# Attention and routed experts on one core: logits in groups of four pairs, wide products from the second expert on, the last two evictions halved

## The chip, the core and the metric

The kernel runs on one core of a Trainium2 chip. The core has a matrix engine (PE), a vector engine (DVE), a scalar engine (ACT), a general engine (POOL) and a queue engine (SP), and 16 DMA engines that move data between HBM and the on-chip memory. PE writes only to PSUM; ACT and DVE read PSUM and write the on-chip memory. The metric is the device time of one execution in microseconds (us).

## What is computed

Causal attention over 4 batches of 12 heads with 448 tokens and head size 64; its rows are the input `x` of a mixture of 8 experts, in which every expert takes 224 tokens.

```
scores = scale * q @ k.T, masked above the diagonal, softmax over keys
x      = (softmax @ v), heads side by side          # 1792 x 768
logits = x @ w_gate                                 # 1792 x 8
order  = argsort(-logits.flatten())                 # greedy: a token to its best expert
...                                                 # that still has room (224 places)
h      = relu(x[mask] @ w1[e]);  out[mask] = h @ w2[e]
```

## The kernel before

**Attention.** The 48 heads are worked as 24 pairs `pp` (6 in a batch), and a batch's 448 tokens as 4 blocks of 112. `plan` writes PE's order out by hand: in round `n` PE computes the scores of pair `n`, the transposes of the softmax of pair `n-1` (`turns`), for early pairs the transposes of the output rows of pair `n-3` (`rows_at`), what `logits_back` adds, the product with `v` of pair `n-1` (`values`) and what `logits` adds for pair `n-2`. Every PE task hangs on the one before (`self.line`), so this order is fixed. DVE and ACT tasks are placed by a planner that works with estimated durations and priorities; some copies may go to either engine (`ACT/DVE`), whichever the planner finds free. Masking with the row maximum (L228) is DVE's, the exponential (L238) ACT's, and copies from PSUM (L252 on ACT, L254 on DVE) are shared.

**Logits.** `w_gate` stands in `WG` as 32 columns for each pair (16 used). `logits_mm` (L331) multiplies the attention output `XT` of several pairs of one batch, each into its own 32 partitions of one PSUM tile: pairs 0 to 3 in one set, pairs 4 and 5 in another. The result is copied out (`lt`), turned back by four transposes (`logits_tr`, L352), and `logits_ev` multiplies on DVE by the reciprocal sums of the softmax (two instructions, L365) and adds over the pairs (L369, and L371 into `L`). The last two pairs go by `logits_direct` (L340), without the way back. In all there are seven sets: 4, 2, 4, 2, 4, 2, 4 pairs, and the direct one.

**Routing.** When `L` of the first three batches is done (`self.log`), DVE may begin with routing steps of low priority, the list `extras`: an argmax over 12 blocks (L632 to L640), keys (L650 to L660) and six comparisons into `Ge` (L674), which PE then sums in `early_count` (L697). After the last batch the router finds, for one expert after the other, the 224 tokens, by rounds in which DVE compares (L668, L783) and PE counts (L769, L786). While the first expert's tokens are looked for, PE runs products without use (L1147).

**Experts.** A second planner orders the eight experts `p`. POOL gathers the 224 rows of an expert (L1129, into one of two `xio` buffers), PE turns them (L1155), ACT and DVE split them into a high and a low part (`xhl`). Weights come in eight pieces for each expert; ACT casts the high part (`wh`, L1114) and DVE subtracts three times for the low part (`wl`, L1120), up to eight pieces ahead. The first product takes 8 blocks `f` of 6 slices `d` each. Expert 0 does it in full precision. From expert 1 on a slice is high times high, high times low and low times high. Expert 1 computes each with 224 columns (L1192, L1193, L1194) into one sum. Experts from `TWICE` on, 2 and later, take both halves of `xhl` in one product of 448 columns (L1190) and then L1194; ACT then copies out the second sum (`hc`, L1204) and DVE adds the two (`hs`, L1208), before ACT's relu (L1200) and DVE's low part (L1212). The second product (L1224) is evicted by ACT (L1228, 384 columns each) into `xio`, and POOL scatters the rows (L1243). The last expert's second product is ordered so that its two last PSUM tiles (`u` 1, `z` 0 and 1) finish one after the other, each with an eviction and a scatter of its own.

Of the kernel before, what the change touches and what calls it, by code (L numbers as in the profile page):

```python
# [7 lines left out]
F32 = mybir.dt.float32  # L8
# [6 lines left out]
OP = mybir.AluOpType  # L15
# [4 lines left out]
C, NC = 112, 4  # L20
# [11 lines left out]
FILL = 0.217  # L32
BIG = 1.0e30
# [3 lines left out]
TWICE = 2  # L37
# [117 lines left out]
class Attention(Schedule):  # L155
    def __init__(self, ctx, tc, gc, keep, k, qk, vP, wgP, xd, L):
# [10 lines left out]
        self.T, self.lt, self.u = {}, {}, {}  # L167
# [159 lines left out]
    def logits_mm(self, b, half):  # L327
        p0, m = ((0, 4), (4, 2))[half]
        t = self.ps.tile([128, S], F32, name="t", bufs=4)
        for p in range(m):  # L330
            self.nc.tensor.matmul(t[32 * p:32 * p + 32], self.WG[:, p0 + p, :], self.XT[6 * b + p0 + p],  # L331
                                  start=True, stop=True)
        self.T["l"] = t

    def logits_direct(self, pp):
        b, q = divmod(pp, 6)
        if q == 4:
            self.u = self.ps.tile([C, NC, 128], F32, name="t", bufs=4)
        for i in range(NC):
            self.nc.tensor.matmul(self.u[:, i, 32 * (q - 4):32 * (q - 4) + 32], self.XT[pp][:, i * C:i * C + C],  # L340
                                  self.WG[:, q, :], start=True, stop=True)

    def logits_cp(self, e, b, half):
        m = (4, 2)[half]
        self.lt = self.wk.tile([128, S], F32, name="lt", bufs=2)
        self.copy(e, self.lt[:32 * m], self.T["l"][:32 * m])

    def logits_tr(self, b, half):
        m = (4, 2)[half]
        self.u = self.ps.tile([C, NC, 128], F32, name="t", bufs=4)  # L350
        for i in range(NC):
            self.nc.tensor.transpose(self.u[:, i, :32 * m], self.lt[:32 * m, i * C:i * C + C],  # L352
                                     self.k["idf"][:32 * m, :32 * m])

    def logits_ev(self, b, half):
        p0, m = ((0, 4), (4, 2))[half]
        if half == 0:
            self.pl = self.wk.tile([C, NC, E, 14], F32, name="pl", bufs=2)
            self.nc.gpsimd.memset(self.pl[:, :, :, 13:14], 0.0)
        pl = self.pl  # L360
        rs = self.RS[b][:, p0:p0 + m, :2 * NC].rearrange("p r (s i) -> p s i r", s=2)
        u = self.u[:, :, :32 * m].rearrange("p i (r z) -> p i r z", z=32)
        o = 9 * half
        for sd in range(2):
            self.nc.vector.tensor_tensor(pl[:, :, :, o + sd:o + 2 * m:2].rearrange("p i e r -> p i r e"),  # L365
                                         u[:, :, :, sd * E:sd * E + E],
                                         rs[:, sd, :, :, None].to_broadcast([C, NC, m, E]), op=OP.mult)
        if half == 0:
            self.nc.vector.tensor_reduce(pl[:, :, :, 8], pl[:, :, :, :8], axis=AX.X, op=OP.add)  # L369
        else:  # L370
            self.nc.vector.tensor_reduce(self.L[:, b * NC:b * NC + NC, :], pl[:, :, :, 8:14], axis=AX.X, op=OP.add)  # L371
# [6 lines left out]
    def plan(self, rt):  # L378
# [4 lines left out]
        self.line = None  # L383
# [129 lines left out]
    def logits(self, pp):  # L513
# [7 lines left out]
        if q not in (3, 5) or not 0 <= pp < NP:  # L521
            return
        half = q // 4
        p0, m = ((0, 4), (4, 2))[half]
        pr = 5.9 - 0.1 * pp
        t = self.pe(0.77, lambda: self.logits_mm(b, half),
                    [self.xts[6 * b + p0 + u] for u in range(m)] + self.ring("t", 4), 3)
        c = self.add("ACT/DVE", {"ACT": 0.42, "DVE": 0.56}, lambda e: self.logits_cp(e, b, half), [t], pr + 0.3)
        self.rings.setdefault("t", []).append([c])
        self.lts = c  # L530

    def logits_back(self, pp):
        b, q = divmod(pp, 6)
# [756 lines left out]
```

## Time and profile before

| | |
|---|---|
| three runs | 498.94, 499.57, 504.29 us; median 499.57 us |
| the profiled execution | 499.02 us, of which the span from first to last instruction is 497.2 us |
| PE busy | 487.1 us, 98% of the span, granted clock 0.997 on average |
| DVE busy | 381.0 us, 77% |
| ACT busy | 305.4 us, 61% |
| POOL busy | 50.2 us, 10% |

Busy time is summed over overlapping matmuls as a union; a matmul's own duration covers its pipeline, so the distance from one start to the next tells what a matmul costs in a stream.

### The profile page before, as it was taken

How to read it: one execution, taken by the hardware profiler on the slowest of the kernel's cores; microseconds unless marked ns; L12 is line 12 of the kernel's file. 1: busy time of each engine (PE TensorE's matmuls, PEld its weight loads, DVE VectorE, ACT ScalarE, POOL GpSimd, SP SyncE). 2: the span in 40 equal slices, each digit the busy share in tenths (PEclk: the TensorE clock that was granted, in tenths of full speed). 3: DMA queues.
4: the chain of work that ended last, by engine and by line, in shares of the span. 5: the costliest groups of instructions: out<-in, count | busy, mean ns of one | idle time of the engine just before them, and what ended most of it. 6: DMA issues, size and time to landing. Idle time of an engine off the chain costs nothing.

```text
span 497.2 us, 10680 instructions
## 1 busy us (share of the span) xinstructions
PE 487.1 (98%) x3933; PEld 406.3 (82%) x3933; DVE 381.0 (77%) x1292; ACT 305.4 (61%) x786; POOL 50.2 (10%) x87
## 2 busy tenths in 40 slices
PE   8999999999999999999999999999999999999995
PEld 4666666766667676999999999999899999999994
DVE  4878777877789786698999999999998486584510
ACT  4988888879898681344645645563664574664410
POOL 5000000000000011010120110210213110200101
PEclk9999999999999999999999999999999999999998
DMA  8933174127000038686967766582976876682101
GB/s 224 316 99 107 38 248 160 39 86 244 6 3 1 1 120 237 242 250 218 331 204 253 240 193 192 196 286 74 299 248 201 295 246 201 212 274 66 57 1 55
DMA packets 18884, 84.07 MB, mean 169 GB/s; under 512 B 2256, under 2 KB 4816, under 8 KB 18832
## 3 DMA queue, kind: packets, MB, share of 16 engines
q1 hardware_dynamic: 16160, 72.36, 45.1%
q0 software_dynamic: 2672, 11.04, 7.1%
q8 instruction: 31, 0.51, 0.4%
q14 instruction: 21, 0.17, 0.1%
HBM read 72.38 MB, written 11.01 MB: 168 GB/s over the span
## 4 chain that ended last, share of the span: by engine, by line
PE 85%; DVE 4%; DMA 4%; ACT 2%; issue 2%; POOL 2%; POOLq 0%; DVEq 0%; ACTq 0%
PE po L1224 25%; PE ph L1190 11%; PE t L246 10%; PE s L272 10%; PE s L218 7%; PE ph L1194 6%; PE t L218 3%; DMA wr<-in_w 2%; DMA xio<-xd,idx 2%; PE rt L769 2%; PE ph L1185 2%; PE ph L1155 2%; PE t L296 2%; PE t L331 1%; PE ph L1192 1%
## 5 line engine op out<-in xcount | busy, mean ns | idle before, releaser
L1120 DVE TENSOR_TENSOR wl<-wr,wh 128x512 fp32r<-128x512 f32 x180 | 116.6, 683 | 14.9 <-ACT wh L1114 14.9
L1114 ACT CAST wh<-wr 128x1536 fp32r<-128x1536 f32 x60 | 88.8, 1480 | 61.7 <-DMA wr<-in_w 36.3
L238 ACT ACTIVATE P<-Sm,mx 112x224 f32<-112x224 f32 (+2 forms) x192 | 99.1, 523 | 23.2 <-DVE mx L228 23.2
L1190 PE MATMUL ph<-xhl,wh 128*128 128x448 f32 x288 | 94.1, 381 | 0.0
L1194 PE MATMUL ph<-xhl,wl 128*128 128x224 f32 x336 | 89.6, 267 | 0.0
L1224 PE MATMUL po<-wh,HH 128*112 128x384 f32 x256 | 68.3, 343 | 0.0
L1224 PE MATMUL po<-wl,HH 128*112 128x384 f32 x256 | 67.6, 340 | 0.0
L1224 PE MATMUL po<-wh,HL 128*112 128x384 f32 x256 | 67.6, 340 | 0.0
L228 DVE CUSTOM_DVE_ANT_0 Sm<-s,MK 112x448 f32<-112x448 f32 (+1 forms) x144 | 59.7, 464 | 6.5 <-POOL iof L580 5.8
L1194 PEld LDWEIGHTS ph<-xhl,wl 128*128 128x128 f32 x336 | 64.2, 191 | 0.0
L1190 PEld LDWEIGHTS ph<-xhl,wh 128*128 128x128 f32 x288 | 54.1, 188 | 4.8 <-issue 0.4
L246 PE MATMUL t<-idf,P 112*112 112x112 f32 x480 | 52.6, 262 | 0.4 <-ACT P L238 0.4
L272 PE MATMUL s<-PT,v 112*64 112x448 f32 (+3 forms) x384 | 50.6, 405 | 0.0
L246 PEld LDWEIGHTS t<-idf,P 112*112 112x112 f32 x480 | 45.9, 133 | 5.1 <-ACT P L238 1.5
L1224 PEld LDWEIGHTS po<-wl,HH 128*112 128x112 f32 x256 | 43.7, 175 | 0.3
L1224 PEld LDWEIGHTS po<-wh,HL 128*112 128x112 f32 x256 | 43.5, 174 | 0.2
L1224 PEld LDWEIGHTS po<-wh,HH 128*112 128x112 f32 x256 | 43.2, 175 | 0.3
L252 ACT COPY PT<-t 112x448 f32<-112x448 f32 (+1 forms) x109 | 42.7, 465 | 1.2 <-PE t L246 1.1
L218 PE MATMUL s<-raw 64*112 64x112 f32 (+2 forms) x288 | 41.4, 415 | 0.1
L272 PEld LDWEIGHTS s<-PT,v 112*64 112x64 f32 x384 | 23.3, 136 | 21.3 <-issue 10.0
L218 PEld LDWEIGHTS s<-raw 64*112 64x112 f32 x288 | 26.8, 174 | 15.8 <-issue 6.1
L238 ACT ACTIVATION_READ_ACCUMULATOR P<-Sm,mx 112x1 f32 x192 | 37.0, 193 | 0.0
(169 smaller groups left out, 655.1 us busy)
## 6 DMA issues: line engine op xcount, KB each, us to landing
wr<-in_w SPq DMA_DIRECT2D x64, 768.0 KB, 5.2
raw<-in_qk SPq DMA_DIRECT2D x11, 896.0 KB, 10.5
v<-in_v SPq DMA_DIRECT2D x12, 448.0 KB, 6.0
xd<-xio SPq DMA_DIRECT2D x2, 1344.0 KB, 6.5
xd<-xio SPq DMA_DIRECT2D x3, 672.0 KB, 4.1
raw<-in_qk SPq DMA_DIRECT2D x1, 448.0 KB, 4.9
xd<-xio SPq DMA_DIRECT2D x1, 448.0 KB, 3.9
xio<-xd,idx POOLq DMA_INDIRECT x16, 5.0
```

What stands on the lines that cost most here:

```text
L218: self.nc.tensor.matmul(ts[sd][:, o:o + m], q[:, 0, i * C:i * C + C], q[:, 1, :m], start=True, stop=True)
L228: self.nc.vector.tensor_tensor_reduce(Sm[:, QO[i]:QO[i] + m], self.S.pop((pp, sd, i)), self.MK[:, S - m:], -0.125, 3.0e38, OP.add, OP.min, ...
L238: self.nc.scalar.activation(P[:, s], Sm[:, s], AF.Exp, bias=mx[:, i:i + 1], scale=-1.0, accum_out=self.RS[b][:, pr, sd * NC + i:sd * NC + ...
L246: self.nc.tensor.transpose(t[:, o + (i - j) * C:o + (i - j) * C + C], P[:, QO[i] + j * C:QO[i] + j * C + C], self.k["idf"][:C, :C])
L252: self.nc.scalar.copy(out, x)
L272: self.nc.tensor.matmul(self.AV[pp][sd * 64:sd * 64 + 64, j * C:S], self.V[2 * pp + sd][:, j, :], self.PT[pp, sd][:, KO[j]:KO[j] + m], sta ...
L296: self.nc.tensor.transpose(t[:, i * 128:i * 128 + 128], self.XT[pp][:, i * C:i * C + C], self.k["idf"])
L1114: self.nc.scalar.copy(hi, self.R[p, c])
L1120: self.nc.vector.tensor_sub(lo[:, s], self.R[p, c][:, s], hi[:, s].bitcast(F32))
L1190: nc.tensor.matmul(t[:, :2 * CAP], hi[:, s], x[:, d].rearrange("p z t -> p (z t)"), start=d == 0, stop=False)
L1194: nc.tensor.matmul(t[:, :CAP], lo[:, s], x[:, d, 0], start=False, stop=d == 5)
L1224: self.nc.tensor.matmul(self.T[p, "o", u][z][:, :384], a[p][:, f, u * C:u * C + C], w[:, o:o + 384], start=f == 0 and n == 0, stop=f == 7 ...
```

## The change

It does three things. The sets of the logits are no longer cut at batches: `SETS` names runs of four pairs, 0 to 3, 4 to 7, 8 to 11, 12 to 15 and 16 to 19, then pairs 20 and 21, and the direct set 22 and 23. `logits_ev` takes a set apart again where a batch ends or its fifth pair begins. `TWICE` is 1, so expert 1 uses the 448-column product and the two additional steps on ACT and DVE. And the last two evictions are cut into 192 columns for ACT and 192 for DVE.

```diff
+SETS = ((0, 4), (4, 4), (8, 4), (12, 4), (16, 4), (20, 2), (22, 2))
-TWICE = 2
+TWICE = 1
...
-    def logits_mm(self, b, half):
-        p0, m = ((0, 4), (4, 2))[half]
+    def logits_mm(self, p0, m):
         t = self.ps.tile([128, S], F32, name="t", bufs=4)
-        for p in range(m):
-            self.nc.tensor.matmul(t[32 * p:32 * p + 32], self.WG[:, p0 + p, :], self.XT[6 * b + p0 + p],
-                                  start=True, stop=True)
-        self.T["l"] = t
+        for u in range(m):
+            self.nc.tensor.matmul(t[32 * u:32 * u + 32], self.WG[:, (p0 + u) % 6, :], self.XT[p0 + u], start=True, stop=True)
+        self.T["l", p0] = t
...
+    def logits_ev(self, p0, m):
+        parts = [[p0]]
+        for p in range(p0 + 1, p0 + m):
+            if p % 6 in (0, 4):
+                parts.append([])
+            parts[-1].append(p)
+        for ps in parts:
...
+            for sd in range(2):
+                self.nc.vector.tensor_tensor(pl[:, :, :, o + sd:o + 2 * n:2].rearrange("p i e r -> p i r e"),
...
+            if q + n == 4:
+                self.nc.vector.tensor_reduce(pl[:, :, :, 8], pl[:, :, :, :8], axis=AX.X, op=OP.add)
+            elif q + n == 6:
+                self.nc.vector.tensor_reduce(self.L[:, b * NC:b * NC + NC, :], pl[:, :, :, 8:14], axis=AX.X, op=OP.add)
...
-        self.log[b] = d
+                if any(p % 6 == 5 for p in range(p0, p0 + m)):
+                    self.log[pp // 6 if pp % 6 == 5 else pp // 6 - 1] = d
...
             if f == 7:
-                a = [add("ACT", 0.41, lambda p=p, u=u, z=z: self.evict(p, u, z), [prev], 9.0) for z in zs]
+                if p == E - 1 and u == 1:
+                    a = [add(e, 0.3, lambda p=p, u=u, z=z, h=h, c=c: self.evict(p, u, z, h, c), [prev], 9.0)
+                         for z in zs for h, (e, c) in enumerate((("ACT", self.nc.scalar.copy),
+                                                                 ("DVE", self.nc.vector.tensor_copy)))]
+                else:
+                    a = [add("ACT", 0.41, lambda p=p, u=u, z=z: self.evict(p, u, z), [prev], 9.0) for z in zs]
...
+    def evict(self, p, u, z, h=None, copy=None):
+        if h is not None:
+            s = slice(h * 192, h * 192 + 192)
+            copy(self.IO[p][:, 2 + u, z * 384:z * 384 + 384][:, s], self.T[p, "o", u][z][:, s])
+            return
```

Three places in the instruction order. Line numbers of the changed program are up to 13 higher. The first is PE in the round in which the fifth and sixth pair of the first batch had their set (`raw` are q and k, `PT` the turned softmax, `lt` the copied logits). Before:

```order
L272 MATMUL s<-PT,v 64x224 x2
L331 MATMUL t<-xt_265,WG 32x448 x2
L218 MATMUL t<-raw 112x224 x2
L218 MATMUL s<-raw 112x448 x2
L218 MATMUL s<-raw 112x336 x2
L218 MATMUL s<-raw 112x112 x2
L246 MATMUL t<-idf,P 112x112 x20
L296 MATMUL t<-idf,xt_265 112x128 x4
L352 MATMUL t<-idf,lt 112x64 x4
```

And now:

```order
L273 MATMUL s<-PT,v 64x224 x2
L219 MATMUL t<-raw 112x224 x2
L219 MATMUL s<-raw 112x448 x2
L219 MATMUL s<-raw 112x336 x2
L219 MATMUL s<-raw 112x112 x2
L247 MATMUL t<-idf,P 112x112 x20
L297 MATMUL t<-idf,xt_265 112x128 x4
L273 MATMUL s<-PT,v 64x448 x2
```

The product and the four transposes of that set are gone from here; pairs 4 and 5 stand with 6 and 7 two rounds later.

The second place is DVE at the end of attention, from the last reciprocals to the last sums of the logits (`Ge`, `k0f` to `k3f` are early routing steps). Before:

```order
L279 RECIPROCAL rs<-rs 112x9
L254 COPY lt<-t 128x448
L254 COPY PT<-t 112x448
L254 COPY PT<-t 112x224
L365 TENSOR_TENSOR pl<-t,rs 112x4x4x8 x2
L369 TENSOR_REDUCE pl<-pl 112x32
```

And now:

```order
L280 RECIPROCAL rs<-rs 112x9
L654 TENSOR_SCALAR k0f<-m_2216 112x12
L655 TENSOR_TENSOR k1f<-m_2216,k0f 112x12
L662 TENSOR_SCALAR k2f<-k1f 112x12
L664 TENSOR_SCALAR k3f<-k1f 112x12
L678 TENSOR_TENSOR Ge<-m_2216,top 112x256 x5
L255 COPY PT<-t 112x448
L678 TENSOR_TENSOR Ge<-m_2216,top 112x256
L371 TENSOR_TENSOR pl<-t,rs 112x4x2x8 x2
L375 TENSOR_REDUCE pl<-pl 112x32
```

The copy of `lt` went to ACT, and ten early routing steps, which stood one to three rounds earlier, now stand around DVE's last copy of `PT`.

The third place is the end of the program with the semaphores that an instruction waits for in brackets: ACT before, and then ACT and DVE now.

```order
L1204 COPY hc<-ph 128x224 [waits PE_49,Activation_49]
L1200 ACTIVATE HH<-hs 128x224 [waits DVE_49]
L1228 COPY xio<-po_6744 112x384 [waits DMASW4_49,DMASW3_49,DMASW5_49,DMASW2_49,PE_49]
L1228 COPY xio<-po_6745 112x384 [waits PE_49]
L1228 COPY xio<-po_6800 112x384 [waits PE_49]
L1228 COPY xio<-po_6801 112x384 [waits PE_49]
```

```order
L1213 COPY hc<-ph 128x224 [waits PE_49,Activation_49]
L1209 ACTIVATE HH<-hs 128x224 [waits DVE_49]
L1241 COPY xio<-po_6724 112x384 [waits DMASW4_49,DMASW3_49,DMASW5_49,DMASW2_49,PE_49]
L1241 COPY xio<-po_6725 112x384 [waits PE_49]
L1239 COPY xio<-po_6780 112x192 [waits DVE_49]
L1239 COPY xio<-po_6781 112x192 [waits DVE_49]
```

```order
L1217 TENSOR_TENSOR hs<-ph,hc 128x224 [waits Activation_49]
L1221 SCALAR_TENSOR_TENSOR HL<-hs,HH 128x224 [waits Activation_49]
L1239 COPY xio<-po_6780 112x192 [waits DMASW4_49,DMASW3_49,DMASW5_49,DMASW2_49,PE_49]
L1239 COPY xio<-po_6781 112x192 [waits PE_49]
```

The halves on DVE wait for PE; the halves on ACT, which read the same PSUM tile, wait for DVE.

## Rows read from the trace of the kernel before

**Rows 1.** Windows: us; busy PE, PEld, DVE, ACT, POOL; PEclk, DMA share, GB/s

```profile
30.00:60.00 30.00, 30.00 (x248) 19.54 (x246) 23.05 (x93) 24.88 (x87) 0.00 (x0) 1.00 0.21 63
242.00:262.00 20.00, 20.00 (x226) 19.74 (x225) 19.43 (x63) 11.84 (x17) 5.60 (x6) 1.00 0.74 247
```

**Rows 2.** Waits of PE: who for whom, us in total, times, longest

```profile
PE ph L1155 <- DMA xio<-xd,idx: 0.6, 2, 0.4
PE rt L786 <- DVE cd L783: 0.5, 2, 0.3
```

**Rows 3.** Timeline of PE, sets of four and two: start, duration, instruction

```profile
42.60 0.96 PE L331 MATMUL t<-xt,WG 128*32 128x448 f32 x8
43.49 0.64 PE L218 MATMUL t<-raw 64*112 64x224 f32 x4
...
57.55 0.95 PE L331 MATMUL t<-xt,WG 128*32 128x448 f32 x4
58.43 0.64 PE L218 MATMUL t<-raw 64*112 64x224 f32 x4
...
63.20 0.43 PE L352 MATMUL t<-idf,lt 64*112 64x64 f32 x4
63.56 0.97 PE L272 MATMUL s<-PT,v 112*64 112x448 f32 x4
```

**Rows 4.** Timeline of PE, the last set of four turned back, and what follows

```profile
171.26 0.65 PE L352 MATMUL t<-idf,lt 128*112 128x128 f32 x4
171.84 2.11 PE L272 MATMUL s<-PT,v 112*64 112x448 f32 x16
```

**Rows 5.** Timeline of PE, first product of expert 1, then of expert 2

```profile
244.04 0.27 PE L1192 MATMUL ph<-xhl,wh 128*128 128x224 f32 x1
...
246.06 0.30 PE L853 MATMUL rt<-val,oh 112*128 112x2 f16 x6
...
280.53 0.37 PE L1190 MATMUL ph<-xhl,wh 128*128 128x448 f32 x1
...
283.69 0.26 PE L769 MATMUL rt<-A,G 112*128 112x8 bf16 x4
```

**Rows 6.** Groups by line and shape: count, busy us, mean ns, idle before

```profile
L1208 DVE TENSOR_TENSOR hs<-ph,hc 128x224 f32<-128x224 f32 x48 | 18.6, 388 | 19.3 <-ACT hc L1204 18.9
L1204 ACT COPY hc<-ph 128x224 f32<-128x224 f32 x48 | 16.5, 345 | 18.6 <-PE ph L1194 16.5 <-PE rt L781 1.1 <-PE rt L786 0.4
L254 DVE COPY PT<-t 112x448 f32<-112x448 f32 x24 | 15.0, 624 | 5.8 <-PE t L246 5.7
L252 ACT COPY PT<-t 112x448 f32<-112x448 f32 x72 | 33.4, 524 | 1.2 <-PE t L246 1.1
```

**Rows 7.** Groups by line, DVE from 176 to 252.5 us: the subtractions for `wl`

```profile
L1120 DVE TENSOR_TENSOR wl<-wr,wh 128x512 fp32r<-128x512 f32 x27 | 17.4, 680 | 0.3 <-ACT wh L1114 0.3
```

**Rows 8.** Timeline of PE, the second product of expert 1 begins

```profile
260.50 0.41 PE L1224 MATMUL po<-wh,HH 128*112 128x384 f32 x1
```

**Rows 9.** Timeline of DVE at the end of attention

```profile
155.04 1.09 DVE L674 TENSOR_TENSOR Ge<-m,top 112x256 bf16<-112x256 f32 x3
...
169.19 0.21 DVE L279 RECIPROCAL rs<-rs 112x9 f32<-112x9 f32 x1
169.32 0.63 DVE L254 COPY lt<-t 128x448 f32<-128x448 f32 x1
170.58 0.97 DVE L254 COPY PT<-t 112x448 f32<-112x448 f32 x2 [0.64 <-PE t L246]
```

**Rows 10.** Timeline: the halved copy in attention, and the program's end

```profile
174.02 0.35 ACT L252 COPY xt<-s 128x224 f32<-128x224 f32 x1 [2.28 <-PE s L272]
174.40 0.39 DVE L254 COPY xt<-s 128x224 f32<-128x224 f32 x1 [1.40 <-ACT xt L252]
491.33 0.48 ACT L1228 COPY xio<-po 112x384 f32<-112x384 f32 x1 [3.69 <-PE po L1224]
492.09 0.94 POOL L1243 DMA_INDIRECT out<-xio,idh  x1 [3.14 <-ACT xio L1228]
```

More of the change, by code (lines that the diff above doesn't have):

```diff
@@ L337, in logits_direct @@
         if q == 4:
-            self.u = self.ps.tile([C, NC, 128], F32, name="t", bufs=4)
+            self.u[pp] = self.ps.tile([C, NC, 128], F32, name="t", bufs=4)
+        u = self.u[6 * b + 4]
         for i in range(NC):
-            self.nc.tensor.matmul(self.u[:, i, 32 * (q - 4):32 * (q - 4) + 32], self.XT[pp][:, i * C:i * C + C],
+            self.nc.tensor.matmul(u[:, i, 32 * (q - 4):32 * (q - 4) + 32], self.XT[pp][:, i * C:i * C + C],
                                   self.WG[:, q, :], start=True, stop=True)
[L343 to L346, printed above, removed]
@@ L348, in logits_tr, with logits_cp @@
-    def logits_tr(self, b, half):
-        m = (4, 2)[half]
-        self.u = self.ps.tile([C, NC, 128], F32, name="t", bufs=4)
+    def logits_cp(self, e, p0, m):
+        self.lt[p0] = self.wk.tile([128, S], F32, name="lt", bufs=2)
+        self.copy(e, self.lt[p0][:32 * m], self.T.pop(("l", p0))[:32 * m])
+    def logits_tr(self, p0, m):
+        u = self.u[p0] = self.ps.tile([C, NC, 128], F32, name="t", bufs=4)
         for i in range(NC):
-            self.nc.tensor.transpose(self.u[:, i, :32 * m], self.lt[:32 * m, i * C:i * C + C],
+            self.nc.tensor.transpose(u[:, i, :32 * m], self.lt[p0][:32 * m, i * C:i * C + C],
@@ L520, in logits @@
             return
[L521 to L530, printed above, removed]
@@ L532, in logits_back @@
-    def logits_back(self, pp):
-        b, q = divmod(pp, 6)
-        if q not in (3, 5) or not 0 <= pp < NP:
-            return
-        half = q // 4
-        p0, m = ((0, 4), (4, 2))[half]
-        pr = 5.9 - 0.1 * pp
-        if pp == NP - 1:
-            t = self.lts
-        else:
-            t = self.pe(0.43, lambda: self.logits_tr(b, half), [self.lts] + self.ring("t", 4))
-        d = self.add("DVE", (1.1, 1.05)[half], lambda: self.logits_ev(b, half),
-                     [t, self.log.get(b)] + [self.rec[6 * b + p0 + u] for u in range(m)], pr + 0.3)
-        self.rings.setdefault("t", []).append([d])
-        self.log[b] = d
+        for p0, m in SETS:
+            if p0 + m - 1 == pp:
+                pr = 5.9 - 0.1 * pp
+                t = self.pe(0.77, lambda: self.logits_mm(p0, m), [self.xts[p0 + u] for u in range(m)] + self.ring("t", 4), 3)
+                c = self.add("ACT/DVE", {"ACT": 0.42, "DVE": 0.56}, lambda e: self.logits_cp(e, p0, m), [t], pr + 0.3)
+                self.rings.setdefault("t", []).append([c])
+                self.lts = c
+                return
@@ new lines, in logits_back @@
+    def logits_back(self, pp):
+        for p0, m in SETS:
+            if p0 + m - 1 == pp:
+                pr = 5.9 - 0.1 * pp
+                if pp == NP - 1:
+                    t = self.lts
+                else:
+                    t = self.pe(0.43, lambda: self.logits_tr(p0, m), [self.lts] + self.ring("t", 4))
+                d = self.add("DVE", 0.3 * m, lambda: self.logits_ev(p0, m),
+                             [t, self.last_ev] + [self.rec[p0 + u] for u in range(m)], pr + 0.3)
+                self.rings.setdefault("t", []).append([d])
+                self.last_ev = d
+                if any(p % 6 == 5 for p in range(p0, p0 + m)):
+                    self.log[pp // 6 if pp % 6 == 5 else pp // 6 - 1] = d
+                return
```

36 lines of the change are left out of this document (16 added, 20 removed).

## The prediction

> **What bounds the kernel now.** I read the windows first. PE is busy in 30.00 of 30 us of the attention, with DVE at 23.05 and ACT at 24.88 [rows 1]: there PE's own work sets the pace, so a product that disappears from PE's stream should shorten the run by what it occupied. In the first product of expert 1 PE is again busy in 20.00 of 20 us, but DVE has 19.43 [rows 1]. So PE sets the end, with DVE close behind it. Then I read PE's waits: after the route to expert 0 only two kinds are left, up to 0.4 us for the gathered rows of one expert and up to 0.3 us for a routing step of DVE [rows 2]. The granted clock is 1.00 in both windows [rows 1], the upper level of 2.4 GHz. Two stretches are not PE's: the way from the last logits to the first expert's rows, a chain of DVE and PE steps that starts when `L` is complete, and the end, where an eviction, a scatter and its landing follow the last product.
>
> **Logits.** What a set costs PE is the distance from its first start to the start of what follows. The product of a set of four takes 43.49 - 42.60 = 0.89 us and that of a set of two 58.43 - 57.55 = 0.88 us [rows 3]: with two pairs PE spends what it spends on four. The way back takes 171.84 - 171.26 = 0.58 us for four [rows 4] and 63.56 - 63.20 = 0.36 us for two [rows 3]. Before there are four sets of four and three of two: 4 x 1.47 + 3 x 1.24 = 9.60 us. Now there are five of four and one of two: 5 x 1.47 + 1.24 = 8.59 us. **PE saves 1.01 us**, in a stretch where nothing else bounds it. One copy of `lt` goes too; DVE gets four more, smaller multiplications, since three sets are cut in two, which I take as even against that copy.
>
> **Early routing steps.** Batch 2 is now complete with pair 19, two rounds later, so the steps that wait for it move into the last rounds. At the end of attention the instruction order puts four key steps and five comparisons between the last reciprocal and DVE's copy of `PT`, with one more comparison behind. Worked through: the reciprocal begins at 169.19 and the next instruction began at 169.32 [rows 9]. Three comparisons take 1.09 us at most [rows 9], so five take 1.8; the four key steps I put at 0.5 us, an estimate from the 0.13 us between the reciprocal and its follower. The copy of `PT` would then begin at 169.32 + 2.3 = 171.6 and, at 0.62 us [rows 6], end at 172.2, where it could begin at 170.58 before [rows 9]. It is needed by the product with `v` that begins at 171.84, but not at once [rows 4]: `values` begins with block 0, which comes from ACT's copies, and that block is 4 of its 16 matmuls with the longest rows, 448 of 1120 columns for each head, so 2.04 x 448 / 1120 = 0.8 us, which gives 172.6. The copy is late by nothing and has 0.4 us to spare; PE and DVE move ahead together by the microsecond saved, so the distance holds. The comparisons are done near 172.6, well before they are summed after 173.88 [rows 4]. The cover is thin: without it PE would wait for the whole 171.6 - 170.58 = 1.0 us. I take 0, with bounds of 0 and 1.0.
>
> **Expert 1.** Six slices of three products take 246.06 - 244.04 = 2.02 us, 0.337 each; ten slices of a wide and a narrow product take 283.69 - 280.53 = 3.16 us, 0.316 each [rows 5]. There are 8 x 6 = 48 slices: 48 x 0.021 = **1.0 us saved on PE**. In exchange ACT copies eight times (0.345 us) and DVE adds eight times (0.388 us): 2.8 and 3.1 us [rows 6]. ACT has 8 us free in this window; DVE has 0.57 [rows 1], so DVE's weight splitting is pushed back by up to 3.1 us. What covers this is DVE's lead: by 252.5 us it has begun 27 subtractions, nine pieces of weights [rows 7], of which the ninth is the first of expert 1's second product and is used at 260.50 [rows 8]. Its lead is 260.50 - 252.5 - 0.68 = 7.3 us, more than twice 3.1. So I cost these additions at 0; if the cover were gone they would cost 3.1 us.
>
> The Trainium skill (TensorE: Matmul & The Clock Gate, Back-to-back issue gap) gives a matmul at full clock its columns over 2.4 GHz and some 2.5 ns. By it three products of 224 columns take 287.5 ns and a wide one with a narrow one 284.9, an estimate that leaves 0.1 us for 48 slices. The rows above say 0.337 and 0.316, and they decide.
>
> **The end.** The halves of an eviction do not run side by side. In the order given above ACT's half waits for DVE's, and the one halved copy that the trace has shows it: ACT's half runs from 174.02 for 0.35 us, DVE's begins at 174.40 [rows 10]. 192 columns are priced from 224 and 448: ACT 0.35 and 0.524, so 0.33 us; DVE 0.39 and 0.624, so 0.36 us [rows 6, 10]. With 0.03 us between them and some 0.05 more until DVE starts (between nothing and 0.1, an estimate: no row here has DVE after a last product), the eviction takes 0.36 + 0.03 + 0.33 + 0.05 = 0.77 us in place of 0.48 [rows 10]. POOL's scatter follows at 492.09 and everything behind it: **0.3 us lost** for the last tile; the tile before it is hidden under eight blocks of products.
>
> The Trainium skill (PSUM — Partial Sum Buffer, PSUM bank collisions raise a hardware error) says that reads of one bank by two engines must be kept apart in time, at different columns too. The trace agrees, as far as one case can: 174.02 + 0.35 = 174.37 ends before 174.40 starts [rows 10].
>
> **The sum.** 499.02 (the profiled execution; span 497.2) - 1.01 - 1.0 + 0.3 = 497.3 us, a span of 495.5. The profiled execution is 0.55 us under the median of the three runs; I keep the sum and let the range take this in.
>
> **Rivals.**
> *Early steps make PE wait.* If the copy of `PT` is late in the last rounds, PE loses 1.0 us there (worked out above), and the time is 498.3. For it: these steps have less room than before. Against it: 0.4 us of slack in the last round.
> *DVE's additional work reaches PE, and the kernel gets slower.* Place: the routing steps between 242 and 380 us, which DVE works between the splits and which PE waits for in order. PE has already waited 0.3 us for one of them [rows 2]. If all eight additions came to PE, 3.1 us, the time would be 497.3 + 3.1 = 500.4. It decides from the point where DVE's lateness at a routing step exceeds what PE has in hand there; more than 1.7 us of the 3.1 must come through for the kernel to be slower than before. Against it: the splits, which can wait 7.3 us, stand behind the routing steps in priority.
> *The new order takes waits away.* The wait for gathered rows (0.4) and for the routing step (0.3) [rows 2] depend on where the planner puts them, and the planner has laid out everything behind expert 1 anew: 497.3 - 0.7 = 496.6.
> *Columns alone set a slice, and the wide product brings nothing.* Then a slice costs the same in both forms (672 columns either way), expert 1 saves 0.1 and the time is 498.2; the page's gap rule above would have it so. Against it stand the rows of expert 2, which is the same product.
> *The halves run side by side.* The end then gains 0.48 - 0.36 - 0.05 = 0.07 instead of losing 0.3: 496.9. The waits in the order speak against it.
>
> **How the numbers follow.** The forecast, 497.3 with its own range of 496.7 to 498.0 (the 0.3 us by which the terms can be off, and a difference between executions), gets 0.56; early steps 0.11; DVE's additions 0.10; waits gone 0.15; columns alone 0.04; halves side by side 0.04. Of these only the DVE case at its full price goes far. The range reaches from 496.0 (waits gone, and as much again as the terms are off) to 499.4 (early steps late and the median's 0.55 on top, or the additions coming through by two thirds), which leaves out some 0.15. About 1%, 5 us, is what a measurement of this kernel can tell from no change; all these cases lie within it. Faster by over 1% would need 494.6 or less, which no sum reaches: 0.02. Slower by over 1%, above 504.6, needs the additions and a new wait together: 0.04. Within 1%: 0.94.
>
> **What would show it.** Right: five L331 sets of eight records and one of four, the last product with `v` about 1.0 us earlier; slices of expert 1 at 0.316 us; the splits of the weights later against PE by up to 3 us but never waited for; at the end a DVE copy of 0.36 and then an ACT copy of 0.33 with the scatter 0.8 us and more after the last product. Wrong: idle time of PE before the product with `v` in the last two rounds, more than 0.7 us of waits for `cd`, `G` or gathered rows after 242 us, or two copies at the end that overlap.

## The result, and the profile after

The changed kernel takes 497.31 us (median of 20 executions, 495.32 to 498.47); the kernel before, beside it on the same chip, takes 500.53 us (median of 20). The ratio is 0.9916, 95% interval 0.9897 to 0.9934: 0.8% faster, which is within 1%. It is not the quotient of the two medians, which is 0.9936 and lies just outside that interval; by the medians the gain is 3.2 us, by the interval 3.3 to 5.2 us. The ratios here and below leave out the few slow executions, while a median may contain one. The profiled execution took 497.29 us, its span is 495.6 us.

The windows of the changed kernel (columns as in [rows 1]):

```profile
30.00:60.00 30.00, 30.00 (x250) 20.02 (x247) 23.10 (x92) 25.57 (x90) 0.00 (x0) 1.00 0.20 63
242.00:262.00 20.00, 20.00 (x172) 18.62 (x172) 18.76 (x60) 12.96 (x24) 3.76 (x6) 1.00 0.58 188
```

PE is still busy all through. In the second window, where DVE took eight additions more, its busy time did not grow: 18.76 us after 19.43 [rows 1]. Work that was there has left the window. DMA is busy for 0.58 of it, after 0.74.

PE's waits after the change, from the view of waits (who for whom, us in total, times, longest):

```profile
PE ph L1164 <- DMA xio<-xd,idx: 1.3, 2, 0.8
PE rt L773 <- DVE G L672: 0.6, 1, 0.6
...
PE ph L1164 <- DVE hs L1217: 0.4, 1, 0.4
...
PE rt L790 <- DVE cd L787: 0.2, 1, 0.2
```

They are larger than those of [rows 2], and yet the kernel is faster. PE's timeline has the sets of the logits; the first is at the place of the first in [rows 3], and the last set, of two pairs, is turned back just ahead of the last full product with `v`:

```profile
42.80 0.96 PE L331 MATMUL t<-xt,WG 128*32 128x448 f32 x8
43.69 0.64 PE L219 MATMUL t<-raw 64*112 64x224 f32 x4
...
169.68 0.43 PE L350 MATMUL t<-idf,lt 64*112 64x64 f32 x4
170.04 2.11 PE L273 MATMUL s<-PT,v 112*64 112x448 f32 x16
```

A set of four still takes 0.89 us. The product that began at 171.84 [rows 4] now begins at 170.04. DVE in these last rounds, to be read beside [rows 9]:

```profile
168.11 0.17 DVE L664 TENSOR_SCALAR k3f<-k1f 112x12 int32<-112x12 int32 x1
168.18 1.76 DVE L678 TENSOR_TENSOR Ge<-m,top 112x256 bf16<-112x256 f32 x5
169.86 0.61 DVE L255 COPY PT<-t 112x448 f32<-112x448 f32 x1
170.40 0.41 DVE L678 TENSOR_TENSOR Ge<-m,top 112x256 bf16<-112x256 f32 x1
```

The five comparisons take 1.76 us. The copy of `PT` ends at 170.47 us; block 0 of PE's product lasts to 170.04 + 0.8 = 170.84. PE is not held up.

In the first product of expert 1 (timeline of PE) a slice is now a wide and a narrow product; from 242.71 to 244.61 there are six:

```profile
242.71 0.38 PE L1199 MATMUL ph<-xhl,wh 128*128 128x448 f32 x1
242.92 0.26 PE L1203 MATMUL ph<-xhl,wl 128*128 128x224 f32 x1
...
244.61 0.56 PE L857 MATMUL rt<-val,oh 112*128 112x2 f16 x16
...
253.97 0.56 PE L773 MATMUL rt<-A,G 112*128 112x8 bf16 x16
...
257.75 0.60 PE L1233 MATMUL po<-wh,HH 128*112 128x384 f32 x2
```

That is 1.90 / 6 = 0.317 us a slice, after 0.337 [rows 5]. The second product begins at 257.75 us, after 260.50 [rows 8]. Ahead of it there is now one routing round (products with `G`, then with `cd`), where the kernel before has two (timeline of PE, before):

```profile
253.25 0.56 PE L769 MATMUL rt<-A,G 112*128 112x8 bf16 x16
...
257.89 0.56 PE L769 MATMUL rt<-A,G 112*128 112x8 bf16 x16
```

The end, beside [rows 10]:

```profile
489.16 0.34 PE L1233 MATMUL po<-wh,HL 128*112 128x384 f32 x1
489.53 0.36 DVE L1239 COPY xio<-po 112x192 f32<-112x192 f32 x1 [3.81 <-PE po L1233]
489.93 0.32 ACT L1239 COPY xio<-po 112x192 f32<-112x192 f32 x1 [3.85 <-DVE xio L1239]
490.52 0.94 POOL L1256 DMA_INDIRECT out<-xio,idh  x1 [3.13 <-ACT xio L1239]
```

From the last product's start to the scatter there are 1.36 us.

To see where the time went I cut two profiles of each kernel at the same instructions of PE. The second profile of each is one of the experiments below. All rows are starts read from PE's timeline, in us.

| from, to | before | before again | after | after again |
|---|---|---|---|---|
| start, to the second wait in the first transposes | 12.05 | 12.60 | 12.25 | 12.27 |
| attention, to the first sum of `Ge` | 163.43 | 163.41 | 161.42 | 161.45 |
| routing and expert 0, to its last product | 66.59 | 66.47 | 67.14 | 67.51 |
| first product of expert 1, to its second | 18.44 | 18.44 | 16.93 | 16.93 |
| to the last product of expert 7 | 230.46 | 231.90 | 231.41 | 230.50 |
| the end | 6.22 | 6.22 | 6.43 | 6.47 |
| span | 497.2 | 499.0 | 495.6 | 495.1 |

Two stages hold to 0.03 us from one execution to another, and they carry the gain: the attention 2.0 us, the first product of expert 1 1.5 us. The attention takes 161.42 to 161.46 us in all nine profiles of this document that have the new sets. Of the 1.5 us, the 48 slices gave 1.06 (16.56 to 15.50 us in sum); 0.46 is the routing round that now stands behind this stretch and has only moved. The end loses 0.2 us. Expert 0 and the experts behind vary by up to 1.4 us between executions of one kernel.

### The profile page after: what moved, and what is told of

Same layout as the page of the kernel before. It is cut to its first block, busy times and chain, and to the rows that moved or that the text cites. A ratio compares the mean times of both kernels' runs of the same rounds, so it can differ in the third digit from the quotient of the medians.

```text
span 495.6 us, 10599 instructions
## 1 busy us (share of the span) xinstructions
PE 484.3 (98%) x3881; PEld 403.7 (81%) x3881; DVE 382.5 (77%) x1301; ACT 308.5 (62%) x798; POOL 49.7 (10%) x87
## 4 chain that ended last, share of the span: by engine, by line
PE 82%; DVE 7%; DMA 5%; ACT 2%; issue 2%; POOL 2%; POOLq 0%; DVEq 0%; ACTq 0%
PE po L1233 21%; PE ph L1199 13%; PE t L247 10%; PE s L273 10%; PE s L219 7%; PE ph L1203 6%; PE ph L1194 3%; DMA wr<-in_w 3%; PE t L219 3%; DMA xio<-xd,idx 2%; PE rt L773 2%; DVE wl L1129 2%; PE t L297 2%; PE ph L1164 1%; PE po L1194 1%
## 5 line engine op out<-in xcount | busy, mean ns | idle before, releaser
L1199 PE MATMUL ph<-xhl,wh 128*128 128x448 f32 x336 | 109.6, 380 | 0.0
L1199 PEld LDWEIGHTS ph<-xhl,wh 128*128 128x128 f32 x336 | 63.2, 188 | 5.3
L253 ACT COPY PT<-t 112x448 f32<-112x448 f32 (+1 forms) x114 | 43.7, 458 | 0.2 <-PE t L247 0.2
L1217 DVE TENSOR_TENSOR hs<-ph,hc 128x224 f32<-128x224 f32 x56 | 21.7, 388 | 20.1 <-ACT hc L1213 15.9
```

The source lines that it names most:

```text
L253: self.nc.scalar.copy(out, x)
L1199: nc.tensor.matmul(t[:, :2 * CAP], hi[:, s], x[:, d].rearrange("p z t -> p (z t)"), start=d == 0, stop=False)
L1217: self.nc.vector.tensor_tensor(t, self.P[p, f][:, :CAP], self.Hc.pop((p, f)), op=OP.add)
```

## The experiments

**Each part alone.** Four kernels on one chip; beside them the kernel before has a median of 500.93 us (28 executions).

The sets alone, without the wide product and with whole evictions (of the edit to the kernel before, which has the new logits code whole, one line and the unchanged `TWICE`):

```diff
+SETS = ((0, 4), (4, 4), (8, 4), (12, 4), (16, 4), (20, 2), (22, 2))
...
 TWICE = 2
...
```

> The sets of the logits alone, everything else as before. By the terms: PE reaches the first transposes of the late rows 1.0 us earlier than before (176.22), if the product and the way back of one set are all that goes, and 1.8 us earlier if the waits of the transposes in three rounds go with them, as in the changed kernel (174.42). Behind it the order is that of before, so the whole time falls by 1.0 to 1.8 us against the runs of before beside it. Rival, early steps make PE wait: the product with v in the last round begins later than 171.84 minus 1.0, and the time falls by less than 0.8.

Measured: 498.58 us, ratio 0.9945 (0.9916 to 0.9974). The attention is as short as in the changed kernel, 161.45 us, but PE waited for gathered rows, 0.9 us of it for those of expert 2:

```profile
PE ph L1159 <- DMA xio<-xd,idx: 1.3, 2, 0.9
PE ph L1159 <- DVE hs L1212: 0.7, 2, 0.4
```

The time fell by 2.4 us by the medians, more than the 1.0 to 1.8 expected, in an interval of 1.3 to 4.2. So the whole 2.0 us of the attention belong to the sets, and one late gather can take nearly half as much.

The wide product alone:

```diff
-TWICE = 2
+TWICE = 1
```

> The wide product for expert 1 alone. By the terms: the attention ends as before (first late rows at 176.2), the first product of expert 1 shrinks from 18.44 us by 1.0 to 1.5 and the time by 0.5 to 1.5, depending on the waits that the new order brings. Rival, the additional work of DVE reaches PE: waits of PE for comparisons and counts after 242 us grow by over 1.7 us and the time does not fall.

Measured: 500.02 us, ratio 0.9966 (0.9941 to 0.9991). The first product of expert 1 takes 16.92 us: the 1.5 us belong to the wide product.

The halves alone:

```diff
-                a = [add("ACT", 0.41, lambda p=p, u=u, z=z: self.evict(p, u, z), [prev], 9.0) for z in zs]
+                if p == E - 1 and u == 1:
+                    a = [add(e, 0.3, lambda p=p, u=u, z=z, h=h, c=c: self.evict(p, u, z, h, c), [prev], 9.0)
+                         for z in zs for h, (e, c) in enumerate((("ACT", self.nc.scalar.copy),
+                                                                 ("DVE", self.nc.vector.tensor_copy)))]
+                else:
...
```

> The halved last evictions alone. By the term: from the start of the last product to the last scatter 1.36 us, as in the changed kernel, in place of 1.13 before: 0.23 us slower in the profile, not to be told from no change in the times. Rival, the halves run side by side: 1.06 us and two copies that overlap.

Measured: 501.73 us, ratio 1.0028 (0.9996 to 1.0059). Its last product starts at 493.13 us, and then (timeline of the end):

```profile
493.51 0.36 DVE L1235 COPY xio<-po 112x192 f32<-112x192 f32 x1 [3.81 <-PE po L1229]
493.90 0.32 ACT L1235 COPY xio<-po 112x192 f32<-112x192 f32 x1 [3.85 <-DVE xio L1235]
494.49 0.94 POOL L1252 DMA_INDIRECT out<-xio,idh  x1 [3.14 <-ACT xio L1235]
```

That is 1.36 us to the scatter again, where whole evictions take 492.09 - 490.96 = 1.13. The halves cost 0.23 us; the other profiles agree, 1.36 us in all eight with halves and 1.13 in all six with whole evictions. The rest of what this execution was longer by stood ahead of the end, in an order that is that of the kernel before.

Sets and wide product, with whole evictions:

```diff
+SETS = ((0, 4), (4, 4), (8, 4), (12, 4), (16, 4), (20, 2), (22, 2))
...
-TWICE = 2
+TWICE = 1
...
```

> The changed kernel without the halved evictions. By the terms it ends 0.23 us sooner than the changed kernel: from the start of the last product to the last scatter 1.13 us, span 495.4 if all else falls as in the changed kernel's profile (495.6). If the parts add up, its gain over before is the sum of the gains of the two kernels with one part each. Rival: the gain of the medians of the changed kernel, 3.2 us, is not in the two parts, and this one gains under 1.5.

Measured: 496.84 us, ratio 0.9917 (0.9885 to 0.9948). It is the fastest median of the four. By the medians the sets alone gain 2.4 us, the wide product alone 0.9 and both together 4.1; the intervals are some 1.3 to 1.6 us wide to either side, so that the parts add up as far as can be told. Its distance to the changed kernel is too small to be told by the medians, but the profile of the end says what the halves cost, so this is the version to keep.

**Controls.** The two kernels unchanged, for a second profile of each. Beside them the kernel before has a median of 500.68 us.

First the kernel before, with no line changed:

> The kernel before, unchanged: a control. Theory 1 (what differs between two profiled executions of one instruction order is when scatters and gathers land, and PE's waits for gathered rows with it): the time is that of before within 0.2%, PE waits again at the turns of gathered rows (L1155) and once or twice for a routing step, 0.8 to 2.5 us together, but by other amounts at each place than the profile of before shows (there 0.17 before the rows of expert 0, 0.3 for expert 2's); the attention, which waits for no DMA in its second half, ends at the same time within 0.3 us (the last sets turned back at 171.3 and the rows behind them at 176.2). Theory 2 (these waits are fixed by the order, so the ones that the changed kernel has anew come from its order): every wait of PE over 0.1 us comes back at its place within 0.1 us.

Measured: 500.92 us, ratio 1.0026 (0.9988 to 1.0063).

```profile
PE ph L1155 <- DMA xio<-xd,idx: 1.9, 3, 1.2
...
PE rt L786 <- DVE cd L783: 0.5, 2, 0.3
```

The waits for routing steps come back as they were [rows 2]. Those for gathered rows went from 0.6 to 1.9 us; one of them, for expert 2, took 1.17 us. The attention is 163.41 us against 163.43.

Then the changed kernel, with no line changed:

> The changed kernel, unchanged: a control for the runs beside it and a second profile. Theory 1 (landings vary from execution to execution): the time is that of the changed kernel within 0.2%, the attention ends within 0.3 us of its first profile (rows behind the last sets at 174.4), the eight additions and the end take what they took (halves 0.36 and 0.32 us), while the waits of PE for gathered rows (0.78 us before those of expert 0, 0.35 and 0.51 later) and the 0.6 us for a G near 230 us come back by other amounts. Theory 2 (the changed order sets them): they come back within 0.1 us.

Measured: 496.71 us, ratio 0.9945 (0.9911 to 0.9980). Attention and expert 1 come back to 0.03 us. The waits in the stage of expert 0 come back by other amounts, and one of 0.67 us for a `cd` near 210 us had not been there. So the small waits of that stage are not what the change did; the table's fixed stages are. Of late gathers more is said at the end of this section.

**Where the second microsecond of the attention came from.** The sets take away 1.06 us of products: from one start to the next, the products of the sets fall from 6.18 to 5.32 us in sum and the ways back from 3.31 to 3.11. The transposes of the softmax, of which there are as many as before, fell by 0.74 us; the other 0.2 us went, half and half, from the transposes of the output rows and the products of q and k. Here the early routing steps are held back in the kernel before:

```diff
-        b3 = [self.log[b] for b in range(B - 1)]
+        b3 = [self.log[b] for b in range(B - 1)] + [self.pts[21, 1, 1]]
```

> The kernel before, with the early routing steps held back until the softmax of pair 21 is copied, as late as the changed sets hold them back; nothing else is touched. In every profile of the order of before (two of that kernel and two with one other part changed) PE's slot for the transposes of one round takes 2.06 us, but 2.11 in the round at 145 us, 2.21 at 151 and 2.33 at 158, and 2.40 at 104; with the changed sets all are 2.06 to 2.14. Theory A (the early steps stand before DVE's copies of these rounds and make PE wait): the slots at 145, 151 and 158 fall to 2.06 each, 0.45 us in sum, the one at 104 stays 2.40, and the attention ends 0.45 us earlier, measured from the first transposes at 12 us on; a time 0.4 us under the kernel before, not to be told from it by the medians. Theory B (the sets of two themselves, with their copy and their two more steps on DVE, make PE wait): the slots stay as they are. Theory C (the steps make PE wait wherever they stand): 0.4 us of waits come up in the last rounds after 164 us instead.

Measured: 500.14 us beside 501.46, ratio 0.9960 (0.9933 to 0.9988). The attention took 162.88 us, 0.55 less than before. PE's timeline of one round, first in the second profile of the kernel before, then in this one:

```profile
158.21 2.40 PE L246 MATMUL t<-idf,P 112*112 112x112 f32 x20
160.54 1.25 PE L272 MATMUL s<-PT,v 112*64 112x448 f32 x6
```

```profile
157.53 2.13 PE L246 MATMUL t<-idf,P 112*112 112x112 f32 x20
159.58 1.25 PE L272 MATMUL s<-PT,v 112*64 112x448 f32 x6
```

The same 20 transposes take 2.33 us from their start to the next instruction, and 2.05 without the early steps in DVE's way; the round before it falls from 2.22 to 2.06. The round at 145 us kept its 2.11, which the expectation had wrong, and no other round took over the wait. So the early steps had cost PE some 0.45 us at their old place, and in the last rounds they cost nothing. How they did it is not isolated: where they stood, the planner had also given DVE three of the six copies of `PT` of each of these two rounds, and with the steps away it gives DVE one. The round at 104 us keeps its 2.39 here and is at 2.11 with the new sets; that 0.3 us goes with the sets of two themselves, and what in them is not isolated.

**What covers DVE's additions.** The prediction said: the lead of the weight splits. In the changed kernel the first subtractions that expert 1's second product needs end at 254.64 us, and that product begins at 257.75, so 7.5 us of lead have become 3.1. If that is the cover, eight more additions should be nearly free and sixteen should not.

```diff
-        self.nc.vector.tensor_tensor(t, self.P[p, f][:, :CAP], self.Hc.pop((p, f)), op=OP.add)
+        for _ in range(2 if p == 1 else 1):
+            self.nc.vector.tensor_tensor(t, self.P[p, f][:, :CAP], self.Hc[p, f], op=OP.add)
```

> The changed kernel, with DVE's addition hs computed twice for each of expert 1's eight blocks (the same result written again), nothing else moved: 8 more additions, 2.4 us of DVE at the distance from one start to the next (0.30) or 3.1 at their full duration (0.388). In the changed kernel the first subtractions for expert 1's second product end 3.1 us before PE uses them (7.5 us in the kernel before). Lead theory: seven of the eight come ahead of these subtractions and take 2.1 to 2.7 us of the 3.1, so PE does not wait for wl and the time is that of the changed kernel within 0.5 us (some 497 to 498 us). No-cover theory: DVE's work reaches PE through the routing steps that PE waits for; 2.4 to 3.1 us more, some 500 us, with the waits of PE for cd and G grown by as much.

Measured: 499.19 us, ratio 0.9971 (0.9950 to 0.9992); the span is 2.3 us longer than that of the control beside it, 1.36 of them in expert 1's first product (18.29 us after 16.93) and 0.6 in a wait for `hs` just behind it. The lead theory falls. PE's waits from 240 to 264 us, where the changed kernel has none:

```profile
PE ph L1164 <- DVE hs L1218: 0.6, 1, 0.6
PE rt L773 <- DVE G L672: 0.5, 1, 0.5
PE rt L790 <- DVE cd L787: 0.3, 1, 0.3
```

The splits were still 2.6 us early. What ran out was a routing step. DVE's second half of `G`, first in the changed kernel, then here:

```profile
252.43 0.55 DVE L672 TENSOR_TENSOR G<-kr,kk 112x768 bf16<-112x768 int16 x1
```

```profile
253.93 0.55 DVE L672 TENSOR_TENSOR G<-kr,kk 112x768 bf16<-112x768 int16 x1
```

Counted from PE's product with `oh` (244.61 and 244.23), `G` is begun after 7.82 and after 9.70 us: 1.9 us later, for five more additions that stand ahead of it. PE comes for it after 9.36 us in both. `G` was ready after 7.82 + 0.55 = 8.37 us, and its second half is used about 0.25 us into the sixteen products, so it had 9.36 + 0.25 - 8.37 = 1.2 us in hand, not 3.1.

Against the run before, the sums three times:

```diff
-        for _ in range(2 if p == 1 else 1):
+        for _ in range(3 if p == 1 else 1):
```

> As the run with the sums computed twice, but three times: 16 more additions, 4.8 to 6.2 us of DVE. Lead theory: fourteen of them, 4.2 to 5.3 us, come ahead of the first subtractions for expert 1's second product, more than the 3.1 us they have in hand, so PE now waits 1 to 2.2 us for wl before that product (near 258 us) and the time is 1 to 2.5 us above that of the changed kernel. No-cover theory: 4.8 to 6.2 us above it. If DVE's work is covered by more than the lead (it sits idle elsewhere): no change.

Measured: 502.98 us, ratio 1.0056 (1.0030 to 1.0082), a span of 501.2 us, 6.1 more than the control's (5.6 of them in expert 1's first product), for at most 6.2 us of DVE. PE never waited for a split. It waited 1.18 us for `hs` (the sum has to be read before its PSUM can be written again) and 1.13 for `G`, and then the windows show (columns as in [rows 1]):

```profile
250.00:254.00 4.00, 3.14 (x20) 2.71 (x19) 3.69 (x17) 2.25 (x4) 2.00 (x3) 1.00 0.40 108
254.00:258.00 4.00, 2.55 (x25) 2.30 (x26) 3.86 (x11) 1.01 (x3) 0.00 (x0) 0.81 0.20 72
258.00:262.00 4.00, 4.00 (x15) 3.51 (x15) 3.90 (x12) 1.08 (x3) 0.00 (x0) 0.50 0.48 154
262.00:266.00 4.00, 4.00 (x41) 3.77 (x40) 3.93 (x12) 1.32 (x5) 0.00 (x0) 0.84 0.10 43
```

PE was idle for some 2.3 us of the first eight. Near the end of its second wait, at about 256.5 us, the granted clock fell to 0.50, the lower level of 1.2 GHz, and stayed there until about 263.3: the windows' means of 0.81, 0.50 and 0.84 make 1.5 + 4 + 1.3 = 6.8 us. Slices start 0.585 us apart there (257.77, 258.35, 258.94) and not 0.317: nine of them cost 2.4 us, as much as the waits.

Why then were the first eight additions free? Counted in PE's instruction order, the routing product that needs `G` stands behind 20 slices of expert 1 (counted from the products with `oh`) in the kernel before, and behind 28 in the changed one. The planner knew of the additions and put it later. In the run with the sums twice it did not know. The next two kernels separate this. First the sums computed twice, with the planner told of them (its line alone is shown):

```diff
-                deps = [add("DVE", 0.31, lambda p=p, f=f: self.mid_sum(p, f), [c] + (hl[-2:-1] if f else []), 8.0)]
+                deps = [add("DVE", 0.62 if p == 1 else 0.31, lambda p=p, f=f: self.mid_sum(p, f), [c] + (hl[-2:-1] if f else []), 8.0)]
```

> As the run with expert 1's sums computed twice, and the planner is told: 0.62 us instead of 0.31 for each of the eight. It now lays out PE's next routing product (L773) behind 34 slices of expert 1's product, where the changed kernel has 28 and the kernel before 20. Theory of the order (what covers DVE's additions is where the planner puts PE's routing products; it had moved them for the change, and could not for the additions that it was not told of): PE's two waits at 254 and 256 us (0.54 and 0.34 in the run that was not planned) are gone or under 0.2 together, expert 1's first product is as long as in the changed kernel within 0.3 us, and the time is 1 to 2.4 us under that run, 497 to 498 us. Theory of a full engine (DVE has nothing in hand in this stretch, the additions reach PE at another place): as that run within 0.7 us, some 499 us, with waits for G, cd or hs of as much further on.

Measured: 498.41 us beside 501.46, ratio 0.9936 (0.9903 to 0.9969). The product stands behind 34 slices, PE does not wait for `G` or `cd` between 240 and 264 us, and expert 1's first product takes 16.91 us, as in the changed kernel, where the unplanned run took 18.29. In this stretch the theory of the order holds. The time does not show it: it is above the 497 to 498 us expected, and the span is only 0.7 us under that of the unplanned run; PE waited 1.40 us for the rows of expert 7 in this execution.

And the changed kernel, whose planner is told of hardly any time for the additions that it has:

```diff
-                deps = [add("DVE", 0.31, lambda p=p, f=f: self.mid_sum(p, f), [c] + (hl[-2:-1] if f else []), 8.0)]
+                deps = [add("DVE", 0.01 if p == 1 else 0.31, lambda p=p, f=f: self.mid_sum(p, f), [c] + (hl[-2:-1] if f else []), 8.0)]
```

> The changed kernel, with the planner told that expert 1's additions take 0.01 us instead of 0.31; they are all computed. The planner then puts PE's routing product behind 21 slices of expert 1's product, about where the kernel before has it (20), not behind 28. Theory of the order: DVE reaches the comparisons G of that round some 2 us later than this order takes for granted, PE waits 0.8 to 2.5 us for G and cd between 250 and 262 us, and the time is 0.8 to 2.5 us above the changed kernel, about 498.3 to 499.8. Lead theory, that of the prediction (only the subtractions for the weights are pushed back, and they have 3.1 us in hand): no such wait, the time of the changed kernel within 0.5 us.

Measured: 500.01 us, ratio 0.9973 (0.9939 to 1.0007). The time is just above the 498.3 to 499.8 that the theory of the order said, and the cause is another: the wait for `cd` is 0.2 us, and DVE came in time for `G`, with nothing in hand. Counted from the products with `oh`, the second half of `G` is done after 7.38 us, and PE, which comes after 7.14, uses it at about 7.39. With the product seven slices earlier only four additions stand ahead of that `G`, not five, so that DVE too is there 1.0 us sooner; that was not in the expectation. PE waited for the rows of expert 2, 1.30 and 0.79 us. So it was run again, with no line changed:

> The run with the planner told 0.01 us for expert 1's additions, once more, for a second profile. Its first profile had PE wait 1.30 and 0.79 us for the gathered rows of expert 2 (at 259.7 and 261.7 us, behind a gather of 2.52 us on POOL) and lose the upper clock for some 3 us, and only 0.2 us for a routing step. Chance theory (that gather was late as one was in the second profile of the kernel before, where PE waited 1.17): these waits are under 0.5 us now, expert 1's first product and the turn behind it take some 17.5 us from the end of expert 0's second product (19.4 in the first profile, 16.9 in the changed kernel), and PE waits for G and cd by 0.2 to 0.6 us. Order theory (this order calls for the rows before they can be there): PE waits there for over 1 us again. In both the median is 499.5 to 500.5 us; what the 2 to 3 us above the changed kernel are made of, if the gather is in time, is to be read from the stages.

Measured: 499.35 us, ratio 0.9963 (0.9936 to 0.9990). The wait came again; PE's waits from 240 to 264 us:

```profile
PE ph L1164 <- DMA xio<-xd,idx: 2.0, 2, 1.8
PE rt L790 <- DVE cd L787: 0.2, 1, 0.2
```

The profiled executions of this order, 501.71 and 503.40 us, are both longer than its medians, 500.01 and 499.35. The first gather for expert 2 on POOL and the next load of weights on SP (timelines: start, duration), with the landing of that gather (DMA view: count, median us from issue to landing), first in the changed kernel, then in this run:

```profile
251.02 0.96 POOL L1138 DMA_INDIRECT xio<-xd,idx  x1 [7.14 <-DVE HL L1221]
254.76 0.33 SPq L1117 DMA_DIRECT2D wr<-in_w  x1
xio<-xd,idx POOLq DMA_INDIRECT x1, 3.7
```

```profile
251.37 1.57 POOL L1138 DMA_INDIRECT xio<-xd,idx  x1 [7.63 <-DVE G L672]
251.92 0.33 SPq L1117 DMA_DIRECT2D wr<-in_w  x1
xio<-xd,idx POOLq DMA_INDIRECT x1, 8.0
```

All fourteen profiles fall into two groups by this:

| first gather for expert 2 | four profiles: before again, the sets alone, both of the unplanned order | the ten others |
|---|---|---|
| next load starts after it by | 0.3 to 1.5 us | 2.5 to 8.4 us |
| its own time on POOL | 1.57 to 2.52 us | 0.96 us |
| lands after its start by | 6.1 to 8.4 us | 3.5 to 3.8 us |
| PE's longest wait for these rows | 0.9 to 1.8 us | none listed |

The gather starts 0.8 us after the last scatter of expert 0 has landed, and that varies: in the kernel before the scatter took 5.7 us to land in one profile and 7.0 in the other. How close the next load stands is also set by the order. The unplanned order, as that of before, has the splits early (7.6 us of lead in its first profile), so the weight buffers come free early. The rows were late in both profiles of the unplanned order, in two of five with the order of before (20 slices), and in none of seven with the product behind 28 or 34 slices. So chance has a part beside the order. That it is the loads that delay the gather is read from the traces, not isolated by an edit. The second gathers do not divide so cleanly: with a load 1.2 to 1.4 us behind their start they landed in 4.4, 5.3 and 6.9 us. And a rival is not tested: DVE's subtraction that frees the load's buffer runs beside the gather in the same four profiles, and the gather's instruction on POOL is itself longer there.

## Why the prediction was right, and where it was not

The time, 497.3, and the class, within 1%, came out. The working was off on two sides, which cancelled by luck.

**The base.** The sum was made against one profiled execution of 499.02 us. The three executions then known had a median of 499.57; twenty have 500.53. So the base was 1.5 us too low; of this the prediction let its range take in 0.55.

**The sum.** It had 1.7 us of gain. The table's fixed stages have 2.0 + 1.5 - 0.2 = 3.3, of which 0.46 only moved to a later stage; what is gone is 2.0 + 1.06 - 0.23 = 2.8. So the sum had 1.1 us too little gain on a base 1.5 us too low. The measured gain, 3.2 us by the medians and 3.3 to 5.2 by the ratio, can't decide what the later stages, which vary by 1.4 us, add to it.

*Logits, 1.01 us:* right; 0.86 and 0.20 are gone from the sets' products and ways back.

*Early routing steps, 0:* right at their new place: the copy of `PT` has 170.84 - 170.47 = 0.4 us to spare, the figure of the prediction. Wrong at the old place: their removal from there was priced at nothing, and it gave 0.45 us. With the 0.3 us at 104 us this is 0.74 of the 1.0 us that the prediction missed in the attention. The trace of before had it: the row of 20 transposes is 2.40 us long there and 2.13 elsewhere. It was overlooked because PE's busy share read 30.00 of 30 and was taken for the absence of waits; matmuls overlap, so waits of up to 0.34 us hid in their durations.

*Expert 1, 1.0 us on PE:* the slices are right (0.317 for a forecast of 0.316). The stage gained 1.5 because one of two routing rounds moved behind the stretch's end; in the later stage it costs again, where 0.5 us can't be told from what executions differ by. The Trainium skill (TensorE: Matmul & The Clock Gate, Back-to-back issue gap) would have left 0.1 us by the rule that the prediction took from it (an estimate; the wide slice comes to 285.0 ns by it, not 284.9), and the changed kernel's rows disagree with that as those of before did. The section gives the rule for an isolated matmul and says that with few columns it counts too little, since it leaves out the weight loads; a slice has two of those now and had three.

*Additional work of DVE, 0:* right in its result; its reason is half of it. The splits did fall back, from 7.5 to 3.1 us, and never made PE wait, even with sixteen further additions. But what ran out first was the routing step `G`, with 1.2 us in hand, as the rival had named the place. The planner had put the product that needs it eight slices later; seven slices earlier nothing was in hand, and PE waited 0.2 us for `cd`. Eight further additions that the planner was not told of cost 1.4 us in the stretch and 2.3 in the span; eight that it was told of cost nothing in the stretch.

*The end, 0.3 us:* 0.23. The halves took 0.36 and 0.32 us with 0.04 between; the 0.05 that DVE was to start later did not show, since DVE begins 0.37 us after the last product's start, as ACT did. The Trainium skill (PSUM — Partial Sum Buffer, PSUM bank collisions raise a hardware error) has reads of one bank by two engines kept apart; the trace agrees again, 489.53 + 0.36 = 489.89 before 489.93, as the program's own waits make it; no run here lets the two meet.

*The rivals.* Waits were taken away by the new order, as one rival had it, but by other waits than it named: the 0.4 and 0.3 us of [rows 2] came back at other places, and those that went were never listed as waits.

## What to carry to other kernels

Before a stage is called free of waits, compare equal groups of it, round by round: 20 transposes of 2.40 us among others of 2.13 are a wait that no view lists. Work added to an engine that is not the bottleneck is paid where another engine comes for its next result, so measure what that result has in hand in the order as the planner will lay it out, not the lead of work with low priority. And take the base from several executions: a stage that repeats to 0.03 us tells a gain better than medians that differ by 1.5.

## What was not expected of the hardware

With the sums computed three times PE had two waits of 1.1 to 1.2 us within 4 us; in the second the granted clock fell to 0.50 and stayed there for some 6.8 us, and nine slices at that level cost 2.4 us more. So the repeated additions at twice the count cost 5.6 us in expert 1's first product, not twice 1.4. In both profiles of the run with unplanned sums, where PE waited 2 us for the rows of expert 2, the clock fell likewise, to 0.66 and 0.65 on average in the 4 us from 262. A gather whose next weight load came 0.3 to 1.5 us behind it landed in 6.1 to 8.4 us, and in 3.5 to 3.8 us where the load came 2.5 us behind it or later; the order with the splits held up is one of those with the load later.
